# First batch turned on TensorE head by head, weight loads spread over it, last pair of each batch in halves

## The chip, the cores and the metric

The kernel runs on one core of a Trainium2 chip. The metric is the device time of one execution in microseconds; the median of three runs is compared. The core's engines work side by side, each through its own queue in order: PE (TensorE), DVE (VectorE), ACT (ScalarE), POOL (GpSimd) and SP (SyncE, which here only issues DMAs).

## The reference

Clustered attention, and behind it a gated feed-forward layer (FFN) on the attention's output:

```python
# q, k, v: (4 batches, 8 heads, 768, 64); centroids: (8, 16, 64)
q_assign = argmax(normalised q . normalised centroids)      # 16 clusters per head
k_assign = argmax(normalised k . normalised centroids)
mask   = q_assign[:, :, :, None] == k_assign[:, :, None, :]
scores = where(mask, q @ k.T / 8, -1e9)
attn   = softmax(scores) @ v
x      = attn, heads side by side                           # (3072 tokens, 512)
out    = (sigmoid(x @ w_gate) * (x @ w_val)) @ w_out         # d_ff = 1536
```

## The kernel before

**Operands.** For each head the kernel wants a tile `T` that holds k and q turned, features down the partitions and tokens along the row: six chunks of 128 keys and six of 128 queries. Each value is split in a high fp16 part and a low one (tile `hl`: DVE casts, then DVE or POOL subtracts), and both parts are turned together. From `T` PE computes the tokens' products with the centroids (`logits`, `logits2`); DVE picks the largest of the 16 and writes a one-hot row (`pick`, tile `oh`); the one-hots are turned too and placed in rows 64 to 79 of `T`, over the low part, with -1920 at the clusters a query is not in. A score matmul of 80 rows then contains the mask.

**Steps.** A step is one block of 128 keys against 384 queries of a head: `do_scores` (line 419: one matmul; line 424: the exponential on ACT), and two steps later (`LA = 2`) `do_av`, three matmuls of 65 columns (line 436). There are 96 steps in a batch, 384 in all. After a head's last step `normalise` divides (DVE, then POOL), and after a pair of heads the result `x` is turned by a DMA into `xT`, the input of the FFN.

**What runs between steps.** `at(i, f)` books preparation at step i, and it is issued in program order behind that step. Batches 1 to 3 are prepared by `pair_prep`, with DMA transposes of `hl` and of the one-hots and DMA copies (`hop`) that place them.

**The first batch before the change.** It is done in two passes of 48 steps: "A" takes all keys and the first 384 queries of every head, "B" the other 384 queries. So the first half of the batch's tokens is ready for the FFN after 48 steps (it starts 12 steps later). `a_split`, `a_turn` (DMA transpose, line 222), `a_logits`, `a_pick` and `a_place` prepare A, `b_split` to `b_place` prepare B. Before the first step 26 dummy matmuls (line 489) run on PE.

**The FFN** is a queue of atoms: 12 pairs of gate and value (lines 301 and 316, four matmuls of 384 columns each, booked at 643 ns apiece) and 9 output atoms (line 333, four matmuls of 512 columns, 864 ns) for each half batch of 384 tokens, which comes to 24 x 643 + 9 x 864 = 23,208 ns. `ffn_run(ns)` issues atoms until its credit is used. Before, the credit per step is the backlog, less a reserve of 7,000 ns, over the steps that are left in the batch:

```python
ffn_run(max(0.0, backlog() - reserve) / (total - done))
```

FFN weights come as float32 and are cast by POOL's DMAs: eight of gate and value, two of output. They are issued at steps 14, 26, 30, 34 (two each), 40 and 46.

**PSUM** has a ring of four banks (scores, logits, gates, values), two for `av`, two for the FFN's output.

Of the kernel before, what the change touches and what calls it, by code (L numbers as in the profile page):

```python
# [16 lines left out]
def kernel(  # L17
# [55 lines left out]


    ident = const.tile([128, 128], FP, name="ident")
    make_identity(nc, ident)
    identh = const.tile([128, 128], HP, name="identh")
    warm = const.tile([128, 512], HP, name="warm")
    POOL.memset(warm, 0.0)
    ones = const.tile([128, 128], HP, name="ones")  # L80
    POOL.memset(ones, 1.0)
# [9 lines left out]
    RAW = {}  # L91
# [6 lines left out]
    load(SP, "k", 0, 0)  # L98
    load(ACT, "q", 0, 0)
    SP.dma_start(out=cen, in_=centroids.rearrange("h c d -> (h c) d"))  # L100
    load(SP, "k", 0, 1)
    load(ACT, "q", 0, 1)
# [9 lines left out]
    def load_w(i):  # L112
        for t, src in ((wg[i], moe_w_gate), (wv[i], moe_w_val)):
            POOL.dma_start(
                out=t.rearrange("p dc fc f -> p dc (fc f)"),
                in_=src.rearrange("(dc p) (g f) -> p dc g f", p=128, f=WQ * 128)[:, :, i, :],
            )
# [15 lines left out]
    def centroid_a():  # L133
        DVE.tensor_tensor(sq, cen, cen, ALU.mult)
        DVE.tensor_reduce(ss, sq, AX.X, ALU.add)
        ACT.activation(r0, ss, AF.Sqrt)
        ACT.activation(r1, warm[:, 0:1], AF.Exp)

    def centroid_b():
        DVE.tensor_scalar(r0, r0, 1e-6, None, ALU.add)  # L140
        DVE.reciprocal(r0, r0)
        for i in range(2):
            DVE.tensor_scalar(c2[:, i, :], cen, r0, None, ALU.mult)
        ct_ps = bank(128, name="ct_ps")
        PE.transpose(ct_ps, c2.rearrange("p a d -> p (a d)"), ident)
        cv = ct_ps.rearrange("p (h c) -> p h c", c=NCL)
        ACT.copy(cm[:, :, 0, :], cv)
        DVE.tensor_tensor(cm[:, :, 1, :], cv, cm[:, :, 0, :], ALU.subtract)
# [4 lines left out]
    def v_cast(b, p):  # L153
        va = vap.tile([128, 2, NCH, 65], HP, name="va")
        VA[b, p] = va
        POOL.memset(va[:, :, :, 64:65], 1.0)
        POOL.tensor_copy(va[:, :, :, 0:64], RAW["v", b, p])
# [110 lines left out]
    ohs = [const.tile([128, NCH, 128], HP, name=f"oh{i}") for i in range(3)]  # L268
# [23 lines left out]
    def ffn_atoms(xT, t0, n, b, ch):  # L292
# [34 lines left out]
        def outp(t, part, st):  # L327
            def f():
                if part == 0:
                    st.append(op.tile([128, DM], FP, name="o"))  # L330
# [65 lines left out]
    def head_steps(b, p, e, kind):  # L396
        h = 2 * p + e
        if kind == "all":
            t, halves = T[b, h], [(T[b, h], 6), (T[b, h], 9)]
        elif kind == "A":  # L400
            t, halves = T["A", h], [(T["A", h], 6)]
        else:
            t, halves = T["A", h], [(T["B", p], 3 * e)]
        steps = []
        for j in range(NCH):
            for i, (tq, qo) in enumerate(halves):
                steps.append(dict(
                    b=b, p=p, e=e, nq=3 * len(halves), k=t[0:80, j, :],
                    q=tq[0:80, qo : qo + 3, :], j=j, c0=3 * i,
# [17 lines left out]
    def do_av(s, xT):  # L427
# [13 lines left out]
        if last:  # L441
            normalise(av, nq, b, p, e, x[:, :, bass.ts(e, 64)])
            if e == 1:
                SP.dma_start_transpose(
                    out=xT[:, p, :].rearrange("p (c t) -> p c t", t=128),
                    in_=x.rearrange("p c t -> p (c t)"),
                )
# [13 lines left out]
    def run_steps(heads, xT, reserve, xt_ready, lag=8):  # L461

        pend = []
        total = sum(n for n, _ in heads)
        done = 0
        for n, th in heads:
            for s in th():
                do_scores(s)
                pend.append(s)
                if xt_ready and done == lag:  # L470
                    xt_ready()
                if xt_ready and done < lag:
                    ffn_run(backlog() / (lag - done + 1))
                else:
                    ffn_run(max(0.0, backlog() - reserve) / (total - done))
                if len(pend) > LA:
                    do_av(pend.pop(0), xT)
# [3 lines left out]
        while pend:  # L481
            ffn_run(150)
            do_av(pend.pop(0), xT)


# [5 lines left out]
    ahl = {}  # L491

    def a_split(h, eng):
        k_, q_ = RAW["k", 0, h // 2], RAW["q", 0, h // 2]
        ahl[h] = split(9, [(0, k_[:, h % 2]), (6, q_[:, h % 2, 0:3])], eng)

    def a_turn(h):
        turn(("A", h), ahl[h], tp)

    def a_groups(h, side):  # L500
        return [(T["A", h], c, h) for c in (range(6) if side == 0 else range(6, 9))]

    st0 = {}

    def first_logits(e, oh):
        lg = logits2(a_groups(e, 0) + a_groups(e, 1))
        pick(lg, [(0, 6, 1, True, oh_view(oh, 2 * e, 1, 1, 6)),
                  (6, 9, 1, False, oh_view(oh, 2 * e + 1, 1, 1, 3))])

    def first_place(e, oh):  # L510
        ps = bank(NCH * 128, HP, name="oh_ps")
        for c in range(NCH):
            PE.transpose(ps[64 * e : 64 * e + 64, bass.ts(c, 128)], oh[:, c, 64 * e : 64 * e + 64], identh)
        t = T["A", e]
        pv = ps.rearrange("p (c t) -> p c t", t=128)
        DVE.tensor_copy(t[64:80, 0:6, :], pv[64 * e : 64 * e + 16, :, :])
        ACT.copy(t[64:80, 6:9, :], pv[64 * e + 32 : 64 * e + 48, 0:3, :])

    def a_logits(p):
        st0["lg", p] = logits2(sum((a_groups(2 * p + e, s) for s in range(2) for e in range(2)), []))  # L520

    def a_pick(p):
        oh = st0["oh", p] = new_oh()
        pick(st0["lg", p], [(0, 12, 2, True, oh_view(oh, 0, 2, 2, 6)),
                            (12, 18, 2, False, oh_view(oh, 1, 2, 2, 3))])

    def a_place(p):
        ps = oh_turn_pe(st0["oh", p], NCH)
        ot = ohp.tile([128, NCH, 128], HP, tag="ohT", name="ohT")
        DVE.tensor_copy(ot.rearrange("p c t -> p (c t)"), ps)  # L530
        for e in range(2):
            hop(ot, 2 * e, T["A", 2 * p + e], 0, 6)
            hop(ot, 2 * e + 1, T["A", 2 * p + e], 6, 3)

    def b_split(p):
        q_ = RAW["q", 0, p]
        st0["bhl", p] = split(6, [(0, q_[:, 0, 3:6]), (3, q_[:, 1, 3:6])], POOL)

    def b_turn(p):
        turn(("B", p), st0["bhl", p], tbp)  # L540

    def b_logits(p):
        st0["blg", p] = logits2([(T["B", p], c, 2 * p + c // 3) for c in range(6)])

    def b_pick(p):
        oh = st0["boh", p] = new_oh()
        pick(st0["blg", p], [(0, 6, 2, False, oh_view(oh, 0, 2, 1, 3))])

    def b_place(p):
        ps = oh_turn_pe(st0["boh", p], 3)  # L550
        ot = ohp.tile([128, 3, 128], HP, tag="ohT", name="ohT")
        DVE.tensor_copy(ot.rearrange("p c t -> p (c t)"), ps[:, 0:384])
        for e in range(2):
            hop(ot, e, T["B", p], 3 * e, 3)

    dummies(8)
    centroid_a()
    a_split(0, DVE)
    a_turn(0)
    a_split(1, POOL)  # L560
    a_turn(1)
    DVE.tensor_copy(identh, ident)
    centroid_b()
    for i in range(3):
        POOL.memset(ohs[i], 0.0)
    load(POOL, "v", 0, 0)
    load(SP, "k", 0, 2)
    load(SP, "q", 0, 2)
    a_split(2, POOL)
    load(POOL, "v", 0, 1)  # L570
    a_split(3, POOL)
    a_turn(2)
    a_turn(3)
    load(SP, "k", 0, 3)
    load(SP, "q", 0, 3)
    dummies(14)
    oh0 = new_oh()
    first_logits(0, oh0)
    dummies(2)
    first_logits(1, oh0)  # L580
    dummies(2)
    first_place(0, oh0)
    v_cast(0, 0)
    first_place(1, oh0)
    a_split(4, POOL)
    a_split(5, POOL)
    load(POOL, "v", 0, 2)
    load(POOL, "v", 0, 3)
    v_sum_pe(0, 0)

    at(0, lambda: a_logits(1))
    at(1, lambda: a_pick(1))
    at(3, lambda: a_place(1))
    at(4, lambda: (a_turn(4), a_turn(5)))
    at(5, lambda: v_cast(0, 1))
    at(6, lambda: v_sum_pe(0, 1))
    at(7, lambda: a_split(6, POOL))
    at(8, lambda: a_split(7, POOL))
    at(9, lambda: (a_turn(6), a_turn(7)))
    at(12, lambda: a_logits(2))  # L600
    at(13, lambda: a_pick(2))
    at(14, lambda: load_w(0))
    at(15, lambda: a_place(2))
    at(16, lambda: v_cast(0, 2))
    at(17, lambda: v_sum_pe(0, 2))
    at(22, lambda: a_logits(3))
    at(23, lambda: a_pick(3))
    at(25, lambda: a_place(3))
    at(24, lambda: v_cast(0, 3))
    at(26, lambda: v_sum_pe(0, 3))  # L610
    at(26, lambda: load_w(1))
    for p in range(NP):
        s = 20 + 7 * p
        at(s, lambda p=p: b_split(p))
        at(s + 3, lambda p=p: b_turn(p))
        at(s + 14, lambda p=p: b_logits(p))
# [102 lines left out]
```

## Time and profile before

| | |
|---|---|
| median of 3 runs | 379.2 us (379.12 to 381.24) |
| span of the profiled execution | 378.3 us |
| PE busy | 337.0 us, 89% |
| ACT, DVE, POOL busy | 230.4, 176.7, 113.6 us |
| mean granted TensorE clock | 0.932 |
| first score matmul | at 21.1 us |
| first score matmul of batches 1, 2, 3 | at 111.6, 170.9, 247.7 us |
| last score matmul | at 319.4 us |

The profiled execution has no time of its own beside its span; the span lies 0.9 us under the median, so 0.9 us is taken for what lies around it. Busy time of PE is time in which a matmul was under way, not time at PE's full rate: at a granted clock of 0.50 the same matmul takes about twice as long, so a busy stretch at that clock does half the work.

### The profile page before, as it was taken

How to read it: one execution, taken by the hardware profiler on the slowest of the kernel's cores; microseconds unless marked ns; L12 is line 12 of the kernel's file. 1: busy time of each engine (PE TensorE's matmuls, PEld its weight loads, DVE VectorE, ACT ScalarE, POOL GpSimd, SP SyncE). 2: the span in 40 equal slices, each digit the busy share in tenths (PEclk: the TensorE clock that was granted, in tenths of full speed). 3: DMA queues.
4: the chain of work that ended last, by engine and by line, in shares of the span. 5: the costliest groups of instructions: out<-in, count | busy, mean ns of one | idle time of the engine just before them, and what ended most of it. 6: DMA issues, size and time to landing. Idle time of an engine off the chain costs nothing.

```text
span 378.3 us, 8520 instructions
## 1 busy us (share of the span) xinstructions
PE 337.0 (89%) x3177; PEld 205.5 (54%) x3177; DVE 176.7 (47%) x455; ACT 230.4 (61%) x527; POOL 113.6 (30%) x179
## 2 busy tenths in 40 slices
PE   3786955669999989889999999999999999999995
PEld 1354633436655556554666566656665566565552
DVE  3463532225563675662656365635563333242230
ACT  3044744437867878875787778758777787232231
POOL 3756566103342634523242423232401000000000
PEclk9975875559999999999999999999999999999999
DMA  5967999974766976966566539653523120300102
GB/s 186 253 187 150 226 179 197 239 137 144 110 175 143 215 187 126 224 165 174 146 148 177 114 88 231 178 139 81 87 52 73 51 36 2 105 1 30 55 2 83
DMA packets 96858, 50.07 MB, mean 132 GB/s; under 512 B 75376, under 2 KB 93424, under 8 KB 96816
## 3 DMA queue, kind: packets, MB, share of 16 engines
q1 hardware_dynamic: 90032, 42.44, 48.0%
q0 software_dynamic: 6240, 6.29, 9.6%
q10 hardware_dynamic: 544, 0.79, 0.6%
q8 instruction: 25, 0.41, 0.4%
q14 instruction: 17, 0.14, 0.1%
HBM read 28.34 MB, written 6.29 MB: 92 GB/s over the span
## 4 chain that ended last, share of the span: by engine, by line
PE 68%; DMA 14%; DVE 7%; issue 4%; POOL 3%; ACT 1%; SPq 1%; POOLq 0%; DVEq 0%
PE o L333 16%; PE v L316 15%; PE g L301 15%; DMA T<-hl 12%; PE sc L419 11%; PE av L436 6%; PE lg L238 2%; DMA T<-ohT 2%; PE wm L489 2%; DMA cen<-in_centroids_dram 1%; DVE hT L321 1%; POOL hl L215 1%; DVE vs L163 1%; DVE hl L212 1%; DVE t L197 1%
## 5 line engine op out<-in xcount | busy, mean ns | idle before, releaser
L424 ACT ACTIVATE es<-sc 128x384 f16<-128x384 f32 x384 | 174.2, 492 | 67.6 <-PE sc L419 54.5
L419 PE MATMUL sc<-T 80*128 80x384 f16 x384 | 124.3, 348 | 5.8 <-DMA T<-ohT 4.5
L436 PEld LDWEIGHTS <-es 128*128 128x128 f16 x1152 | 84.6, 102 | 51.0 <-ACT es L424 6.1
L436 PE MATMUL av<-va,es 128*128 128x65 f16 x1152 | 102.3, 200 | 1.4 <-ACT es L424 0.7
L321 DVE SCALAR_TENSOR_TENSOR hT<-th,v 128x384 f16<-128x384 f32 x96 | 53.0, 552 | 94.8 <-PE av L436 56.1
L202 POOL TENSOR_TENSOR xp<-t,rec 128x384 f16<-128x384 f32 (+1 forms) x40 | 28.3, 707 | 146.2 <-DVE rec L199 119.2
L333 PE MATMUL o<-wo,hT 128*128 128x512 f16 x288 | 70.3, 378 | 0.0
L307 ACT ACTIVATE th<-g 128x384 f32<-128x384 f32 x96 | 47.2, 492 | 28.5 <-DVE hT L321 16.2
L301 PE MATMUL g<-xTb,wg 128*128 128x384 f16 x288 | 58.6, 325 | 0.5 <-DVE hT L321 0.2
L316 PE MATMUL v<-xTb,wv 128*128 128x384 f16 x288 | 58.6, 325 | 0.3 <-DVE hT L321 0.3
L301 PEld LDWEIGHTS <-wg 128*128 128x128 f16 x384 | 37.7, 98 | 24.0 <-issue 3.8
L316 PEld LDWEIGHTS <-wv 128*128 128x128 f16 x384 | 37.5, 98 | 22.7 <-issue 2.5
L333 PEld LDWEIGHTS <-hT 128*128 128x128 f16 x288 | 27.8, 97 | 26.1
L419 PEld LDWEIGHTS <-T 80*128 80x128 f16 x384 | 38.3, 100 | 5.4 <-DMA T<-ohT 4.2
L632 POOL TENSOR_TENSOR hl<-kraw,hl 128x384 f16<-128x384 f32 x24 | 22.0, 917 | 31.4 <-issue 24.8
L197 DVE TENSOR_TENSOR t<-av,sv 128x390 f32<-128x390 f32 (+1 forms) x40 | 19.2, 479 | 22.9 <-PE av L436 22.9
L632 POOL TENSOR_TENSOR hl<-qraw,hl 128x384 f16<-128x384 f32 x24 | 21.9, 913 | 20.7 <-DVE hl L631 20.5
L342 ACT ACTIVATE ob<-o 128x512 f32<-128x512 f32 x16 | 9.6, 597 | 22.6 <-PE o L333 22.4
L163 DVE TENSOR_REDUCE vs<-vraw 128x128 f16<-128x768 f32 x12 | 17.6, 1466 | 0.0
L340 DVE TENSOR_SCALAR ob<-o 128x512 f32<-128x512 f32 x8 | 5.5, 692 | 25.6 <-PE o L333 25.6
L252 DVE TENSOR_TENSOR lgs<-lg,lglo 128x192 f32<-128x192 f32 x24 | 8.5, 355 | 17.8 <-ACT lglo L244 17.3
L229 PE MATMUL lg<-cm,T 128*128 128x16 f16 x192 | 6.5, 172 | 10.9 <-DMA T<-hl 10.9
(68 smaller groups left out, 241.8 us busy)
## 6 DMA issues: line engine op xcount, KB each, us to landing
kraw<-in_k_dram SPq DMA_DIRECT2D x16, 384.0 KB, 3.9
out_dram<-ob SPq DMA_DIRECT2D x24, 256.0 KB, 2.1
qraw<-in_q_dram SPq DMA_DIRECT2D x14, 384.0 KB, 4.1
vraw<-in_v_dram SPq DMA_DIRECT2D x12, 384.0 KB, 5.4
vraw<-in_v_dram POOLq DMA_DIRECT2D x4, 384.0 KB, 4.4
wg<-in_moe_w_gate_dram POOLq DMA_DIRECT2D x4, 384.0 KB, 8.2
wv<-in_moe_w_val_dram POOLq DMA_DIRECT2D x4, 384.0 KB, 9.6
wo<-in_moe_w_out_dram POOLq DMA_DIRECT2D x2, 768.0 KB, 13.6
```

The lines of the kernel that those rows point to most:

```text
L163: DVE.tensor_reduce(s[:, :, 0:64], RAW["v", b, p].rearrange("p h c d -> p h d c"), AX.X, ALU.add)
L197: DVE.tensor_tensor(t[:, 0:nq, :], av, sv, ALU.add)
L202: (eng or POOL).tensor_tensor(x, t[:, 0:nq, 0:64], bcast(rec[:, 0:nq], 64), ALU.mult)
L301: PE.matmul(out=g[:, 0:n], lhsT=wg[fc // WQ][:, dc, fc % WQ, :], rhs=xT[:, dc, t0 : t0 + n], start=(dc == 0), stop=(dc == NDC - 1),)
L307: ACT.activation(th[:, 0:n], g[:, 0:n], AF.Tanh, scale=0.5)
L316: PE.matmul(out=w[:, 0:n], lhsT=wv[fc // WQ][:, dc, fc % WQ, :], rhs=xT[:, dc, t0 : t0 + n], start=(dc == 0), stop=(dc == NDC - 1),)
L321: DVE.scalar_tensor_tensor(hT[:, fc, 0:n], st[0][:, 0:n], 1.0, w[:, 0:n], ALU.add, ALU.mult)
L333: PE.matmul(out=o, lhsT=hT[:, fc, bass.ts(t, 128)], rhs=wo[fc // 6][:, fc % 6, :], start=(fc == 0), stop=(fc == NFC - 1),)
L419: PE.matmul(out=sc.rearrange("p (c t) -> p c t", t=128), lhsT=s["k"], rhs=s["q"], start=True, stop=True,)
L424: ACT.activation(es, sc, AF.Exp, scale=SCALE)
L436: PE.matmul(out=av[:, s["c0"] + i, :], lhsT=s["es"][:, bass.ts(i, 128)], rhs=VA[b, p][:, e, s["j"], :], start=(first and i == 0), stop=(la ...
L632: POOL.tensor_tensor(hl[:, :, 64:128], r, hl[:, :, 0:64], ALU.subtract)
```

## The change

- **First batch.** No A and B passes. Every head of batch 0 gets its 12 steps with all 768 queries, as in the other batches. `pieces(p, e)` prepares a head: casts on DVE, the low part on POOL (`hi`, `lo`), 12 PE transposes in two PSUM tiles (`tu`), DVE copies to `T` (`ev`), 24 logit matmuls (`lg`), the pick (`pk`), six PE transposes of the one-hots (`ot`), and two DVE writes straight into rows 64 to 79 (`pl`). The table `OFF` says how many steps ahead of the head each is issued. The PSUM tiles come from the two banks of the FFN's output, which is idle until late in this batch.
- **Start.** Pair 0 is loaded by heads, and head 0 is prepared in two parts of three chunks; its steps are ordered so that the first three need only the first part. Centroids are loaded first, on ACT's queue; all other loads of the batch go to SP's. 7 dummy matmuls instead of 26.
- **Weights** are issued one DMA at a time, every 10 steps from step 8 on, the output weights at 88 and 98.
- **Last pair of each batch** is done in halves (queries 0 to 383 of both heads, then the rest, 6 steps each), so that the first half of the tokens is complete at step 84 and its FFN is queued at step 92; the second half's FFN is queued at step 8 of the next batch.
- **Pacing.** Each step gives the FFN 500 ns of credit; there is no reserve, and the FFN halves are queued one behind the other (`ffn_block`), not interleaved (`ffn_two`). The last two steps' `av` of a batch now follow the first scores of the next.

```diff
+    def pieces(p, e, parts=1):
...
+        def tu(s, part=0):
+            a, z = rng(s, part)
+            ps = st["ps", s, part] = (
+                turns(name="t_ps") if parts == 1 else bank(128 * (z - a), HP, name="t_ps")
+            )
+            for c in range(a, z):
+                PE.transpose(ps[:, bass.ts(c - a, 128)], st["hl"][:, c, :], identh)
...
+        def pl(s, eng=None, part=0):
+            a, z = rng(s, part)
+            src = st["oh", part][-s][64 * e + 32 * s : 64 * e + 32 * s + 16, 0 : 128 * (z - a)]
+            dst = T[0, h][64:80, a:z, :].rearrange("p c t -> p (c t)")
+            if s == 0:
+                DVE.tensor_copy(dst, src)
+            elif eng is ACT:
+                ACT.activation(dst, src, AF.Copy, scale=MASK)
+            else:
+                DVE.tensor_scalar(dst, src, MASK, None, ALU.mult)
...
+    OFF = dict(hi0=-30, lo0=-30, hi1=-28, lo1=-28, tu0=-21, ev0=-20, tu1=-19, ev1=-18,
+               lg=-15, pk=-14, ot=-10, pl0=-9, pl1=-7)
+    W0, WS = 8, 10
...
+    for i in range(4):
+        for j in range(2):
+            at(W0 + WS * (2 * i + j), lambda i=i, j=j: load_w(i, j))
+    at(W0 + WS * 8, lambda: load_wo(0))
+    at(W0 + WS * 8 + 10, lambda: load_wo(1))
...
-    run_steps(heads(0, "A", 6), xA, 0, None)
-    run_steps(heads(0, "B", 6), xB, 6000, lambda: ffn_block(xA, 0, 384, 0, [0, 1, 2]), lag=12)
...
+                if second and done == LAG:
+                    second()
+                if done == 84 + LAG:
+                    first()
+                ffn_run(FFN_NS)
...
+    LAG = 8
+    FFN_NS = 500.0
...
+    def heads(b):
+        out = [(12, lambda p=p, e=e: head_steps(b, p, e, [0, 1])) for p in range(NP - 1) for e in range(2)]
+        return out + [
+            (6, lambda e=e, c=c: head_steps(b, NP - 1, e, [c])) for c in range(2) for e in range(2)
+        ]
...
+    CH = [[0, 1, 2], [3, 4, 5]]
+    prev = None
+    for b in range(B):
+        xT = xtp.tile([128, NDC, S], HP, tag="xTb", name="xTb")
+        half = lambda i, xT=xT, b=b: ffn_block(xT, 384 * i, 384, b, CH[i])
+        run_steps(heads(b), xT, prev, lambda: half(0))
+        prev = lambda half=half: half(1)
```

In batch 0 the last pair's `x` is turned by PE as well (`turn_x`), five steps after its `av`; elsewhere by DMA as before.

## The prediction

> **What bounds the kernel now.** I read the slices of the page first, then the six stages, then the chain, then PE's rows in the first batch. Slices (9.46 us each):
>
> ```profile
> PE   3786955669999989889999999999999999999995
> ACT  3044744437867878875787778758777787232231
> PEclk9975875559999999999999999999999999999999
> DMA  5967999974766976966566539653523120300102
> ```
>
> PE is full from slice 9 to the end at a granted clock of 9 and more. Before that it is half idle, and half of that time at half clock, while the DMA row is full in slices 4 to 7. So there are two kernels: a PE-bound one from about 85 us on, and a first batch bound by something else. The stages (start, batch 0 in its two passes, batches 1, 2, 3, tail); after the colon-pair come its length, then busy us of PE, PEld, DVE, ACT, POOL, the granted clock, DMA share and GB/s:
>
> ```profile
> 21.10:68.70 47.60, 30.57 (x379) 21.72 (x379) 19.02 (x62) 23.44 (x50) 28.30 (x45) 0.64 1.04 186
> 68.70:111.60 42.90, 38.06 (x372) 24.01 (x370) 21.13 (x63) 27.58 (x64) 10.71 (x17) 0.80 0.72 160
> 111.60:170.90 59.30, 53.00 (x613) 33.44 (x610) 35.51 (x93) 48.21 (x118) 24.45 (x36) 1.00 0.77 178
> 170.90:247.70 76.80, 75.90 (x756) 47.03 (x757) 42.68 (x106) 56.73 (x132) 24.68 (x36) 1.00 0.62 151
> 247.70:319.70 72.00, 71.64 (x688) 44.18 (x685) 31.82 (x74) 54.75 (x127) 14.64 (x23) 1.00 0.33 68
> 319.70:378.30 58.60, 54.78 (x309) 29.39 (x307) 16.28 (x30) 16.01 (x32) 0.83 (x1) 1.00 0.13 45
> ```
>
> Batches 2 and 3 and the tail are PE-bound (75.90 of 76.80, 71.64 of 72.00). Batch 0 takes 90.5 us, more than batch 2, though batch 2 carries 46.4 us of FFN and batch 0 only 17.2 (23.2 less the 6.0 it leaves). The chain names what stands there:
>
> ```profile
> 39.10 4.37 DMA T<-ohT
> ...
> 58.23 21.27 DMA T<-hl x2
> ```
>
> PE waits for DMA-turned operands, in the stretch in which the weights are issued. Last, what the half clock costs and what ends it:
>
> ```profile
> 37.70:41.10 3.40, 3.40 (x30) 2.48 (x29) 1.29 (x4) 2.17 (x5) 0.66 (x1) 0.50 1.26 168
> 41.20:44.60 3.40, 2.64 (x63) 2.12 (x62) 1.88 (x7) 2.10 (x6) 2.33 (x5) 1.00 1.02 228
> 68.40:71.80 3.40, 3.40 (x37) 2.34 (x37) 1.33 (x5) 2.18 (x5) 0.56 (x1) 0.50 1.21 196
> 71.90:75.30 3.40, 2.07 (x26) 1.41 (x25) 1.24 (x5) 1.57 (x4) 0.76 (x2) 0.50 1.14 294
> ```
> ```profile
> 39.78 0.51 PE L419 MATMUL sc<-T 80*128 80x384 f16 x1
> 40.27 0.51 PE L419 MATMUL sc<-T 80*128 80x384 f16 x1
> ...
> 68.36 0.49 PE L229 MATMUL lg<-cm,T 128*128 128x16 f16 x12 [4.64 <-DMA T<-hl]
> 68.71 0.80 PE L419 MATMUL sc<-T 80*128 80x384 f16 x2
> ...
> 69.99 0.51 PE L283 MATMUL oh_ps<-identh,oh 128*128 128x128 f16 x3
> 70.29 0.53 PE L419 MATMUL sc<-T 80*128 80x384 f16 x1
> ```
>
> At half clock a step of one score and three `av` matmuls costs PE 0.49 us (39.78 to 40.27), 12 logit matmuls 0.35 (68.36 to 68.71), three transposes 0.30 to 0.32 (69.99 to 70.29, a score behind them), so 0.105 each. At full clock the same steps follow each other every 0.385 us (scores at 46.67, 47.05, 47.44, 47.82 in the timeline), which is ACT's pace: seven exponentials in 2.89 us.
>
> **The change part by part.**
>
> *Batches 1 to 3 and the tail.* FFN per batch becomes 2.0 us (four steps of 500 ns from step 92) carried back, and 44.4 of the two halves in the batch: 46.4 in each of batches 1, 2 and 3. That is what batch 2 carries now (7.0 taken over, 46.4 queued, 7.0 left), so batches 1 and 2 get its row, 76.8 each, and batch 3 its own, 72.0 (no later batch to prepare). Batch 1 thus grows by 17.5. At the end 21.2 + 23.2 = 44.4 are left instead of 53.4: the tail is 58.6 - 9.0 = 49.6. The x of the last pair's first half must land between its `av` (issued at step 85) and the gate at step 92. The way is 0.36 + 0.18 + 0.52 (rows L197, L199, L202 for 3 chunks) and 3.1 for the DMA, 4.2 us, against four steps of 0.75 and three of 0.39, 4.2 us: I take nothing, and 1 us in each of three batches as the worse end.
>
> *The start (21.1 now).* The 5.75 us of dummies in the chain and the DMA turns go. New chain: centroids land at 5.65 now as the third DMA of SP, and come first on another queue: 5.1. Squares and sum 0.45, cast 0.35 (5.9); reciprocal 0.30, low part in two halves 0.35 each (6.9; POOL's two at 0.57 lie beside it); turn and evacuate two tiles of three, 0.5 + 0.36 x 2 (8.0); centroid tiles 0.29 x 2 (8.6); 12 logits 0.35 (8.9); pick 0.26 + 0.20 x 2 (9.6); six transposes 0.63 and their drain 0.2 (10.4); place 0.36 (10.8). Ten hand-overs at 0.07 make 11.5. ACT's own list (table load 1.28, two copies 0.47, v's cast, bounded by POOL's 0.84) ends at about 9.9, below it. Bounds: 10.5 and 14 (loads of pair 0 not before today's 6.0, and none of the hand-overs hidden). SP now issues 14 loads in a row at about 0.5 each, 7 us, ahead of its first transpose, which is not due before step 25: free.
>
> *Batch 0 on PE, at half clock.* 96 steps x 0.49 = 47.0. Turns of seven heads, 84 x 0.105 = 8.8; one-hots, 48 x 0.105 = 5.0; logits, 7 x 0.70 = 4.9; v's sums, 4 x 0.63 = 2.5 (38.65 to 39.28 in the timeline); batch 1's logits, 4 x 0.46 = 1.8 (288 in 11.0 us); x, three transposes 0.3. Sum 70.3. ACT needs 96 x 0.41 = 39 and lies beside it. DVE: six heads of casts 0.9, evacuations 1.12, pick 0.86, place 0.55 + 0.69, normalise 0.75 and half of sv 0.15, 5.0 each, 30; rests of heads 0 and 1, 7; batch 1's casts, picks and first v sum, 10 x 0.45 + 4 x 1.42 + 1.76 = 12: 49 of 70. POOL: 12 + 10 subtractions at 0.91, x 6.6, v 4, weights and zeros 9: 40. Both have room; at PE's full clock DVE would be the tightest. What DMA loses (12 turns of `hl`, 20 small copies) is gone from PE's waits, not moved: 15.4 us of waits of PE for batch 0's own turns (10.9 on `T<-hl`, 4.5 on `T<-ohT`). The weights, issued every 10 steps, land 8.2 to 9.6 us later (page, DMA issues); the last gate and value at step 78 is due about step 120, the output weights of steps 88 and 98 about step 123. If that cover were gone, PE would wait up to 13.6 us for `wo`. The last pair's x is turned at five steps behind its `av`, 3.6 us, for 1.1 us of DVE and POOL; only scores stand behind it.
>
> *Does PE stay at half clock?* It is at half clock at step 0: 7 dummies are 3.0 us (8 took 3.59), and the start then has gaps. Both windows of 3.40 us above are full of PE. Behind the one, which holds scores, `av` and a v sum, the clock is 1.00; behind the other, which also holds 12 logits and three transposes, it is 0.50. Of a head's 8.8 us at half clock 2.6 are logits and transposes, more than in the second window (0.65 of 3.40, 19%, against 30%), so by that row a full PE doesn't open the gate while heads are being prepared. Preparation ends at step 77; seven steps without any follow, 3.4 us, and the clock should open at about step 82. That takes 0.1 off 12 steps, 1.2, and gives the four FFN atoms their full-clock price, 16 x 0.163 = 2.6. So batch 0 is 70.3 - 1.2 + 2.6 = 71.7. The other end: if transposes count, PE fills a window early, the clock opens, and the batch runs at DVE's and ACT's pace: 12 us for the first 12 steps, in which DVE has 8.8 us of work and PE is still slow, then 84 x 0.53 = 45: 57.
>
> The Trainium skill, "TensorE: Matmul & The Clock Gate", section "Part 4: PE-mode transpose", speaks against this change: in transpose mode PE does not count as busy in the same way, and the full clock does not engage. By that rule batch 0 stays in the slow case; by a gate that counted transposes as any matmul it would be the 57. The row of 68.40 agrees with the rule, but logits stand in it as well, so the trace does not separate the two.
>
> **Sum.** 11.5 + 71.7 + 76.8 + 76.8 + 72.0 + 49.6 = 358.4; with 0.9 outside the span 359.3, say 359, against 379.2: 5% faster. Against now: start -9.6, batch 0 -18.8, batch 1 +17.5, tail -9.0.
>
> **The rivals.**
> 1. *The clock opens early in batch 0* (57 instead of 71.7): 345. For it: PE is nearly full there once prepared operands no longer come by DMA, and 41.20 shows the clock held at 2.64 of 3.40. Against it: 68.40.
> 2. *DMA still late.* Batch 1's turns of `hl` are issued at steps 47 to 95 among weights, loads and x, and the 21.27 us of the chain come back in part: half is 370, all of it 380. For it: 4.7 MB of loads, 3.2 of weights and 2.9 of turns in some 60 us are 180 GB/s, near the 186 of the stretch now. Against it: weights at half of today's density.
> 3. *Slower: DVE's queue is taken in order, and so is PE's.* Each head needs PE, DVE, PE, DVE, PE, DVE: turn 0.63, evacuate 0.56, logits 0.70, pick 0.86, turn 0.63, place 1.24. If this chain is not hidden behind steps but exposed, it is 4.6 us for each of seven heads, 32 us: 391. The point from which it decides is 2.9 us a head (20 us in seven). For it: DVE has 49 us of work in this batch and must not be late once; a logit bank in the ring of four holds up scores until DVE has read it. Against it: `OFF` puts 9 steps (4 to 6 us) between subtraction and turn and 2 to 4 between the links.
> 4. *The change doesn't do what it says*: the halves of the last pair let only 2.0 us of FFN into their own batch. That is in the sum already, and a first batch without FFN is paid for in batch 1.
>
> **How the numbers follow.** Forecast 0.54, rival 1 0.27, rival 2 0.11, rival 3 0.08. The likeliest time is 359, its own range 352 to 367 (start 10.5 to 14, 3 us of x, some exposure of heads). The range for 8 in 10 reaches down over rival 1 (345 less 3) and up over half of rival 2: 342 to 373. A measurement of this kernel tells about 1%, 3.8 us, from no change. Faster by more: the first two cases and half of rival 2, 0.87; same, rival 2 in full and a part of rival 3, 0.06; slower 0.07.
>
> **What would show it.** First score at 11 to 13 us; batch 0 some 72 us long with a granted clock of 0.50 to about step 80 and PE nearly full; no DMA into `T` before batch 1; batches 1 and 2 at 76 to 78 us each with PE full; last score 49 to 50 us before the end. Wrong would be a batch 0 over 91 us (the forecast's break-even), a clock that falls in batch 1, or PE waiting for `xTb` at step 92 by more than 1 us.

## The result, and the profile after

The changed kernel takes 352.25 us (median of four runs, 351.25 to 353.12) against 379.16 for the kernel before: a ratio of 0.928, 95% interval 0.9245 to 0.9315. The forecast was 359.0 with a range of 342 to 373. The profiled execution took 351.25 us, its span is 349.5. Medians are of all runs of a kernel; ratios, here and below, are to the kernel before as it was measured beside that run, and leave out the few executions that were over 1.5% slower than the fastest of the same kernel.

The slices of the page, 8.74 us each:

```profile
PE   7899987898999999999999999999999999999995
ACT  6478766776768876787768866787768766531330
PEclk9699989899999999999999999999999999999999
DMA  7968999999357735767468536951542002101002
```

PE is now nearly full from the first slice on. The clock row (granted TensorE clock, in tenths of full speed) has a 6 in the second slice and an 8 in the sixth and eighth; the fives that the first batch had are gone. The stages (start, batch 0, batches 1, 2, 3, tail; behind each stretch its length, busy us of PE, PEld (TensorE's weight loads), DVE, ACT and POOL with their instructions in brackets, the granted clock, the DMA share and GB/s):

```profile
0.00:9.60 9.60, 6.22 (x51) 3.43 (x51) 4.99 (x20) 6.04 (x11) 4.65 (x16) 1.00 0.76 243
9.60:71.40 61.80, 55.52 (x771) 38.81 (x771) 43.95 (x119) 43.12 (x102) 38.23 (x51) 0.89 0.99 210
71.40:149.00 77.60, 75.61 (x756) 46.53 (x754) 42.68 (x112) 56.79 (x133) 26.05 (x39) 1.00 0.72 162
149.00:226.00 77.00, 75.43 (x752) 46.33 (x749) 42.00 (x111) 56.72 (x133) 25.02 (x38) 1.00 0.65 151
226.00:300.30 74.30, 73.41 (x697) 44.74 (x696) 33.09 (x81) 54.98 (x128) 14.97 (x25) 1.00 0.30 69
300.30:349.50 49.20, 45.14 (x262) 24.76 (x260) 14.66 (x27) 13.93 (x28) 0.51 (x1) 0.98 0.10 35
```

Batch 0 went from 90.5 to 61.8 us, the start from 21.1 to 9.6, the tail from 58.6 to 49.2; batch 1 took over FFN work and grew from 59.3 to 77.6. The clock of batch 0 is 0.89; the forecast had 0.50 to about step 80. The trace has it at full from 6.54 to 9.96, so at step 0 (9.56) too, at half from 9.96 to 16.78, and at full again from there (the clock "opens" when it goes from half to full). Three windows around that opening:

```profile
9.90:13.40 3.50, 3.44 (x43) 2.55 (x42) 2.44 (x6) 1.87 (x4) 3.02 (x4) 0.51 1.06 384
13.40:16.80 3.40, 3.40 (x41) 2.91 (x39) 1.60 (x6) 1.07 (x3) 0.00 (x0) 0.50 1.08 374
16.80:20.20 3.40, 3.14 (x59) 2.22 (x57) 3.02 (x8) 2.40 (x6) 1.90 (x3) 1.00 0.74 260
```

The window from 13.4 is full of PE, with 12 transposes and ten logit matmuls among its 41 instructions, and the clock behind it is 1.00. Steps 0 to 11 take 10.1 us, the next 36 steps 19.4 (6.6, 6.1, 6.7), the last 48 steps 32.3. In these the clock falls twice for 3.4 us, at 47.5 and 61.2, each time after a window in which PE had been short of work (busy for 76% and 58% of it). The chain (the work that ended last, each piece with its start and length) has two landings of batch 1's operands there, at 45.80 and 68.28, and PE's waits in batch 0 (in all, times, longest) have two lines above 1 us that bear on it:

```profile
39.35 6.45 DMA T<-hl
...
62.74 5.54 DMA T<-hl
```
```profile
PE lg L257 <- DMA T<-hl: 1.5, 2, 0.8
PE sc L434 <- DVE T L596: 1.3, 1, 1.3
```

The first landing lies in the window ahead of the first fall. The second comes behind the second fall; ahead of that one stands the 1.3 us wait, at 59.3, for the write of a one-hot by DVE (line 596).

### The profile page after: what moved, and what is told of

The parts are those of the page before. It is cut to its first block, busy times and chain, and to the rows that moved or that the text cites. A ratio compares the mean times of both kernels' runs of the same rounds, so it can differ in the third digit from the quotient of the medians.

```text
span 349.5 us, 8661 instructions
## 1 busy us (share of the span) xinstructions
PE 331.3 (95%) x3272; PEld 204.6 (59%) x3272; DVE 181.4 (52%) x465; ACT 231.6 (66%) x531; POOL 109.4 (31%) x170
## 4 chain that ended last, share of the span: by engine, by line
PE 76%; DVE 9%; DMA 7%; issue 3%; ACT 2%; POOL 1%; POOLq 0%; ACTq 0%; DVEq 0%
PE o L351 17%; PE v L334 17%; PE g L319 15%; PE sc L434 13%; PE av L451 9%; DMA T<-hl 6%; PE lg L257 2%; DVE hT L339 2%; DVE vs L182 2%; ACT es L439 2%; PE t_ps L545 1%; DVE t L216 1%; DVE hl L679 1%; POOL hl L534 1%; PE lg L248 1%
## 5 line engine op out<-in xcount | busy, mean ns | idle before, releaser
L434 PE MATMUL sc<-T 80*128 80x384 f16 x384 | 120.7, 334 | 2.5 <-DVE T L596 1.3
L451 PEld LDWEIGHTS <-es 128*128 128x128 f16 x1152 | 81.5, 99 | 57.1 <-ACT es L439 13.6
L451 PE MATMUL av<-va,es 128*128 128x65 f16 x1152 | 99.7, 196 | 2.5 <-DVE hl L679 0.6
L319 PE MATMUL g<-xTb,wg 128*128 128x384 f16 x384 | 78.6, 325 | 1.6 <-DVE xTb L471 0.4
L334 PE MATMUL v<-xTb,wv 128*128 128x384 f16 x384 | 78.1, 325 | 1.4 <-DVE hT L339 1.4
L351 PE MATMUL o<-wo,hT 128*128 128x512 f16 x288 | 71.3, 378 | 0.0
L434 PEld LDWEIGHTS <-T 80*128 80x128 f16 x384 | 37.6, 98 | 1.4 <-DVE T L592 0.5
L680 POOL TENSOR_TENSOR hl<-qraw,hl 128x384 f16<-128x384 f32 x24 | 21.9, 912 | 11.0 <-DVE hl L679 10.9
L257 PE MATMUL lg<-cm,T 128*128 128x32 f16 x288 | 11.0, 177 | 2.3 <-DMA T<-hl 2.3
L176 POOL CAST va<-vraw 128x768 f16<-128x768 f32 x15 | 13.1, 872 | 0.0
```

What stands on the lines that cost most here:

```text
L319: PE.matmul(out=g[:, 0:n], lhsT=wg[fc // WQ][:, dc, fc % WQ, :], rhs=xT[:, dc, t0 : t0 + n], start=(dc == 0), stop=(dc == NDC - 1),)
L334: PE.matmul(out=w[:, 0:n], lhsT=wv[fc // WQ][:, dc, fc % WQ, :], rhs=xT[:, dc, t0 : t0 + n], start=(dc == 0), stop=(dc == NDC - 1),)
L351: PE.matmul(out=o, lhsT=hT[:, fc, bass.ts(t, 128)], rhs=wo[fc // 6][:, fc % 6, :], start=(fc == 0), stop=(fc == NFC - 1),)
L434: PE.matmul(out=sc.rearrange("p (c t) -> p c t", t=128), lhsT=s["k"], rhs=s["q"], start=True, stop=True,)
L451: PE.matmul(out=av[:, s["c0"] + i, :], lhsT=s["es"][:, bass.ts(i, 128)], rhs=VA[b, p][:, e, s["j"], :], start=(first and i == 0), stop=(la ...
L680: POOL.tensor_tensor(hl[:, :, 64:128], r, hl[:, :, 0:64], ALU.subtract)
```

## The experiments

Three questions: does a PE that transposes open its clock (the step on which forecast and result differ); which parts of the change carry the 27 us; and what still holds batch 0 up. The parts undone one by one are the even issue of the weights, the turns on PE and the halves. The single pass, the new start and the pacing without a reserve were not, so what each of them is worth stays open; and since the parts lean on each other, the losses below don't add up to 27.

### A full PE of three kinds, ahead of the first batch

The 7 dummy matmuls give way to a stream of about 10 us at half clock: 96 transposes, 24 matmuls of 512 columns, or 352 matmuls of 16 columns. Each was run once, and only the clock is read from it.

```diff
-    dummies(7)
+    wt = bank(128, HP, name="wt")
+    for i in range(96):
+        PE.transpose(wt, warm[:, 0:128], identh)
```

Transposes:

> The 7 dummy matmuls ahead of the first batch give way to 96 PE transposes of 128x128 in a row, about 96 x 0.107 = 10.3 us at half clock; everything else stays. Theory A (a PE that is full opens the clock, whatever fills it, as the changed kernel's stretch 13.40:16.80 suggests, full with 12 transposes, logits and scores and followed by clock 1.00): the granted clock goes to 1.00 within 3.4 to 6.9 us of the first transpose, from when on transposes follow each other at about half their distance, and the stream ends near 8 us. Theory B (the forecast's: transposes do not count): the clock stays at 0.50 to the end of the stream, at about 12 us, and opens only after it.

Wide matmuls:

> Control: 24 dummy matmuls of 512 columns in a row (24 x 0.427 = 10.2 us at half clock) in place of the 7. Both theories: the clock opens 3.4 to 6.9 us after the first one; the distance of two matmuls then falls from 0.427 to about 0.216, and the stream ends at 7 to 9 us.

Narrow matmuls:

> 352 matmuls of 16 columns in a row (the form of the logits, about 0.03 us apart: 10.2 us) in place of the 7 dummies. Theory A in its strong form (any instruction on PE counts): the clock opens 3.4 to 6.9 us after the first. Theory A in a weaker form (columns that stream count: 16 columns of 0.03 us are some 0.4 of PE's rate at half clock): it stays at 0.50 to the end. Theory B: it stays at 0.50.

The number of the stream's matmuls that are under way in a window of 1 us (in brackets), and their distance in time, measure the clock. Transposes:

```profile
4.00:5.00 1.00, 1.00 (x13) 1.00 0.80 244
5.00:6.00 1.00, 1.00 (x14) 1.00 1.00 336
6.00:7.00 1.00, 1.00 (x22) 1.00 0.96 346
```

Wide:

```profile
3.00:4.00 1.00, 1.00 (x4) 1.00 0.81 197
6.00:7.00 1.00, 1.00 (x7) 1.00 1.03 329
```

Narrow:

```profile
6.00:7.00 1.00, 1.00 (x44) 1.00 1.08 347
10.00:11.00 1.00, 1.00 (x44) 1.00 1.05 386
```

The number behind the brackets is the granted clock, and it reads 1.00 here from the start: ahead of the first change on record the profile shows full clock, whatever PE runs at, so the counts decide. Transposes started at 1.82 us at 0.107 us from each other and ran at 0.056 from 5.75 on, 3.9 us later, in a stream that held nothing else. Wide matmuls went from 0.427 to 0.216 at 4.5 us, 3.2 us after the first. Theory A holds for transposes, and theory B falls. The narrow stream is at 44 in every window, 0.027 us apart; that says little by itself, since logits of this width are 0.025 apart at full clock in the changed kernel. But the first clock change on record in that kernel is the opening at 27.67 us, head 0's transposes at 16.2 to 17.0 us are still 0.107 apart, and steps 0 to 11 took 10.5 us, so it had not opened before; PE was full of the narrow matmuls from 1.3 to about 7.2 us. So what narrow matmuls alone leave open is whether a longer stream without a break would do; a window full of them did not.

How far can one window be trusted? In all twelve traces the changes of the clock lie multiples of 3.41 us apart (47.50, 50.92, 61.16 and 64.57 in the changed kernel). Of the windows between these times in the first 110 us of each trace, 40 are at half clock with PE busy for at least 99.5%, not counting the one of narrow matmuls alone (ahead of a trace's first change, which is always to full, the clock counts as half). Behind 36 of them the clock was full, behind 4 it was not. The row of 68.40 in the kernel before, on which the forecast leaned, is one of the four; the others are one of the wide stream's kernel (55.7) and two of the kernel with DMA turns (54.8 and 58.2). What sets these four apart is open: windows with as many transposes and logits opened.

### The weights issued in bunches again

```diff
-    for i in range(4):
-        for j in range(2):
-            at(W0 + WS * (2 * i + j), lambda i=i, j=j: load_w(i, j))
-    at(W0 + WS * 8, lambda: load_wo(0))
-    at(W0 + WS * 8 + 10, lambda: load_wo(1))
+    for i, s in enumerate((14, 26, 30, 34)):
+        for j in range(2):
+            at(s, lambda i=i, j=j: load_w(i, j))
+    at(40, lambda: load_wo(0))
+    at(46, lambda: load_wo(1))
```

> The changed kernel with the weight loads back at the steps of the kernel before (14, 26, 30, 34 with two each, 40, 46). If the even issue carries part of the gain (theory: dense weights crowd out batch 1's operand turns, as in the chain of before with 21.27 us): batch 0 grows from 61.8 by 4 to 12 us, the clock falls once more, time 356 to 364. If it was only the first batch's own operands that waited for DMA: batch 0 within 1.5 us, time 351 to 354.

Measured 359.72 us, ratio to the kernel before 0.9482 (0.9435 to 0.953): 7.5 us of the gain are gone. The stage of batch 0, one line of PE's waits in it, and the step of its chain:

```profile
9.20:81.70 72.50, 58.95 (x769) 41.49 (x769) 46.87 (x121) 44.16 (x102) 38.74 (x52) 0.86 0.96 201
```
```profile
PE lg L257 <- DMA T<-hl: 6.9, 3, 6.5
```
```profile
48.05 15.05 DMA T<-hl
```

Batch 0 grew by 10.7 us (the profiled execution is the slowest of the four). The weights collide with batch 1's operands: a turn lands 15 us after its issue, PE waits 6.5 us at once for such a turn, and the clock is at half for 20.5 us in three stretches instead of 6.8 in two after the beginning. So the even issue carries some 7.5 of the 27 us.

### The operands of heads 2 to 7 turned by DMA again

```diff
-    OFF = dict(hi0=-30, lo0=-30, hi1=-28, lo1=-28, tu0=-21, ev0=-20, tu1=-19, ev1=-18,
+    OFF = dict(hi0=-30, lo0=-30, hi1=-28, lo1=-28, dm=-24,
```

Here `dm` is a DMA transpose of the head's `hl` into `T`; the one-hots are still turned on PE.

> The changed kernel with the operands of heads 2 to 7 of the first batch turned by DMA again (issued four steps after the second subtraction, nine steps before the logits); head 0, head 1, the one-hots and all else stay as changed. Removes 72 PE transposes (72 x 0.055 = 4.0 us at full clock) and 12 evacuations (6.7 us of DVE), adds six DMA turns. Theory 1 (PE's turns are what pays): PE waits for the six turns, 1 to 2.5 us each, the clock falls more often, batch 0 +6 to +15 us. Theory 2 (the start, the single pass and the pacing pay; who turns is of no matter): batch 0 within 2 us, or shorter by up to 4.

Measured 368.51 us, ratio 0.967 (0.961 to 0.973): some 15 us of the gain are gone, by the ratios. Batches 0 and 1, and PE's waits from 9 to 100 us:

```profile
9.20:79.10 69.90, 59.67 (x698) 41.56 (x698) 40.67 (x109) 45.46 (x102) 38.24 (x51) 0.73 1.10 219
79.10:167.60 88.50, 78.13 (x755) 47.55 (x754) 42.81 (x112) 56.95 (x133) 26.02 (x39) 0.94 0.78 143
```
```profile
PE lg L257 <- DMA T<-hl: 9.5, 1, 9.5
PE lg L248 <- DMA T<-hl: 8.2, 4, 5.5
```
```profile
80.81 16.12 DMA T<-hl
```

Batch 0 is 8.1 us longer, as theory 1 had it, with 73 fewer PE instructions and 3.3 us less DVE work: saved work that buys nothing, because the turns land late (PE waits 8.2 us for them, L248) and the clock is 0.73. The rest is in batch 1, 10.9 us longer, where PE waits 9.5 us at once for an operand of batch 1 (L257 is the logits of later batches). That one is not shown to come from the six turns: the last of them had landed by 59.3, and the late turn was issued at 80.81. What stands beside it are the loads of the output weights of steps 88 and 98, which landed at 86.5 and 99.5. The same turn (booked at step 95) in all runs, in us:

| run | output weights at steps | that turn, issue to landing | first 12 steps of batch 1 |
|---|---|---|---|
| changed kernel | 88, 98 | 7.6 | 10.4 |
| w1_fill | 88, 98 | 9.3 | 12.2 |
| c2_wide, u2_whole | 88, 98 | 9.6, 9.6 | 12.5, 13.6 |
| c1_turns, x1_act | 88, 98 | 10.5, 10.6 | 13.7, 13.9 |
| c3_narrow | 88, 98 | 12.7 | 16.5 |
| u3_dma | 88, 98 | 16.1 | 20.0 |
| u1_dense | 40, 46 | 5.5 | 9.4 |
| v1_gap, v2_late (below) | 98, 106 | 5.0, 4.4 | 9.4, 9.5 |

Every run with these weights at 88 and 98 loses time at that turn, and no other run of the table does. No run moves these two loads alone, so that they are the cause is argued from the table and not shown; why the turn takes 7.6 us in one and 16.1 in another is open too.

### The last pair of each batch whole

```diff
-    FFN_NS = 500.0
+    FFN_NS = 530.0
...
-        run_steps(heads(b), xT, prev, lambda: half(0))
-        prev = lambda half=half: half(1)
+        run_steps(heads(b), xT, prev, lambda: None)
+        prev = lambda half=half: (half(0), half(1))
```

`heads` gives the last pair two heads of 12 steps, as the other pairs.

> The changed kernel without halves: the last pair of each batch runs head by head with 12 steps, both FFN halves are queued at step 8 of the next batch, and the credit is 530 ns a step instead of 500, so that 88 steps still carry 46.4 us. By the forecast's sums the halves move 2.0 us of FFN from the tail into the first batch and nothing else: time +1 to +3 us, tail 51 instead of 49.2. Rival (the halves matter more, since the FFN's queue runs dry for the first eight steps of each batch and PE has only scores and av): +5 to +9 us.

Measured 373.48 us, ratio 0.9815 (0.9754 to 0.9876): 20 to 21 us of the gain are gone, far over both expectations. Batch 0 is 59.9 us, but batches 1 to 3 take 83.2, 81.1 and 80.3 (77.6, 77.0 and 74.3 with halves) and the tail 57.9 instead of 49.2. Three windows at the beginning of batch 2:

```profile
152.00:156.00 4.00, 3.68 (x36) 1.73 (x36) 1.34 (x5) 4.00 (x11) 2.91 (x5) 1.00 1.09 295
156.00:159.00 3.00, 0.35 (x5) 0.29 (x5) 0.00 (x0) 0.15 (x1) 0.52 (x1) 0.97 0.74 141
159.00:162.20 3.20, 3.20 (x16) 1.61 (x14) 0.55 (x1) 1.47 (x3) 0.00 (x0) 0.50 0.72 109
```

and PE's waits in the tail and, of another kind, in batch 1:

```profile
PE g L319 <- DMA xTb<-xp: 4.1, 1, 4.1
```
```profile
PE lg L257 <- DMA T<-hl: 3.9, 1, 3.9
```

The FFN's queue is dry for the first eight steps of a batch, which then pass at ACT's pace (152 to 156: ACT 4.00 of 4.00). They take some 3 us, too little for the last pair's division and turn: the FFN's first gate matmul stands at the head of PE's queue and waits (156 to 159: PE 0.35 of 3.00), scores and all else behind it. And the clock halves for the next 3.4 us. It waits 2.7 us so in batch 2, 3.4 in batch 3 and 4.1 in the tail, which lose 4.1, 6.0 and 8.7 us. Batch 1, whose `x` came by PE, has no such wait; of its 5.6 us the 3.9 are the late turn of the table above. With halves there is a half of FFN in hand while the other half's operand is turned. (The kernel before had a reserve of 7,000 ns for the same purpose; this experiment has neither, so it does not say what halves would be worth beside a reserve.)

### A fuller start, moved weights, later logits

```diff
-    dummies(7)
+    dummies(8)
...
     a["pk"](0)
+    fill(1)
     a["ot"](0)
+    fill(2)
```

> The changed kernel with four more dummy matmuls in gaps of PE before step 0 (one more at the start, one between the logits and the turn of head 0's one-hots, two behind that turn), so that PE is full from 1.3 to about 9.6 us. If a full PE opens the clock, it is at 1.00 by step 0 and the cold stretch 9.96 to 16.78 goes: steps 0 to 11 take 7.5 to 9 us instead of 10.1, time -1 to -2.5 us (349.8 to 351.3). If transposes do not count, it stays cold to 16 us and the time is the same or up to 0.9 us longer, by what the dummies delay.

Measured 351.73 us, ratio 0.9269 (0.923 to 0.9309), not told apart from the changed kernel; the gain of 1 to 2.5 us was expected and did not come. Yet the start did what it should. First the changed kernel, then this one, each with the first 12 steps and the first 12 steps of batch 1:

```profile
9.60:19.60 10.00, 9.82 (x131) 7.55 (x131) 6.72 (x18) 4.74 (x11) 4.40 (x6) 0.66 1.01 357
71.40:81.80 10.40, 9.55 (x103) 6.25 (x101) 5.40 (x13) 7.43 (x18) 4.18 (x6) 1.00 1.16 196
```
```profile
9.00:17.40 8.40, 7.54 (x133) 5.70 (x132) 7.36 (x20) 4.68 (x11) 4.33 (x6) 1.00 1.06 375
68.70:80.90 12.20, 9.59 (x104) 6.29 (x103) 5.43 (x13) 7.46 (x18) 4.18 (x6) 1.00 1.27 181
```

The clock is full from 6.7 to 44 us, the first 12 steps take 8.4 instead of 10.1 us (8.4 also in both kernels below, which have this start; with the changed kernel's start they took 8.8 to 10.5 in u1_dense, u2_whole and x1_act, so a part of the 1.7 us varies from run to run). Batch 1 begins 2.7 us earlier, and its first 12 steps give 1.8 of that back: an operand turn that PE waits 2.6 us for, the one of the table. It lands at 79.6 us, against 80.5 in the changed kernel, so a faster PE waits longer for nearly the same landing.

So, on top of this start, the weights were moved to where DMA had room (v1_gap, below); and then the logits, pick and one-hot turn of later batches were also put two steps later (v2_late), so that an operand's turn has two steps more:

```diff
-    for i in range(4):
-        for j in range(2):
-            at(W0 + WS * (2 * i + j), lambda i=i, j=j: load_w(i, j))
-    at(W0 + WS * 8, lambda: load_wo(0))
-    at(W0 + WS * 8 + 10, lambda: load_wo(1))
+    for n, s in enumerate((8, 14, 20, 26, 32, 38, 64, 82)):
+        at(s, lambda i=n // 2, j=n % 2: load_w(i, j))
+    at(98, lambda: load_wo(0))
+    at(106, lambda: load_wo(1))
```

> The fuller start (four more dummies) and the weights moved to where DMA has room: gate and value at steps 8, 14, 20, 26, 32, 38, 64 and 82, output weights at 98 and 106. In the changed kernel DMA moves 122 to 125 GB/s from 17 to 35 us and 201 to 255 from 44 to 87, where batch 1's operands are turned. If DMA's crowding between steps 47 and 110 is what gave the fuller start's gain back: PE's waits for turned operands of batch 1 fall below 1 us, the first 12 steps of batch 1 take 9.5 to 10 us instead of 12.2, time 346.5 to 349.5. If batch 0's end is bound by DVE and POOL: 350.5 to 352.

Measured 350.64 us, ratio 0.9254 (0.9223 to 0.9284): the lowest of all, not distinguishable from the changed kernel, and in the second theory's range (350.5 to 352). The first 12 steps of batch 1 take 9.4 us, where 9.5 to 10 was expected of the first theory, but steps 48 to 59 take 8.8 instead of 7.3, and PE's waits for batch 1's operands are not below 1 us; 2.9 of these 3.3 us now lie in batch 0:

```profile
PE lg L257 <- DMA T<-hl: 3.3, 3, 2.2
```

> As the one with the moved weights, and the logits, pick and one-hot turn of batches 1 to 3 come two steps later, so an operand turn has 13 steps instead of 11 before its logits. If turns still land late after the move of the weights: 1 to 2 us less than it, and no falls of the clock in batch 0. If they land in time by then: the same within 0.5 us.

Measured 355.01 us, ratio 0.9374 (0.9346 to 0.9401): worse, which neither theory had.

```profile
PE t_ps L550 <- DVE T L561: 2.5, 3, 1.9
```

The waits for DMA are gone from PE's list, and these 2.5 us of waits for DVE's evacuations have come in (0.6 before); the clock falls three times. Batch 0 took 62.1 us, 0.5 more than with the weights moved alone; batches 1, 2 and 3 took 0.7, 1.1 and 1.3 more, for which no cause was found. That the moved picks meet the first batch's heads in DVE's queue is a guess from the waits.

### The last one-hot write on ACT

```diff
-                f = d[k_[:2]]
+                f = d[k_[:2]] if k_ != "pl1" else (lambda s_, d=d: d["pl"](s_, ACT))
```

> The changed kernel with the last write of each head's one-hots (the queries', 16x768, 0.56 us on DVE) moved to ACT, for heads 2 to 7. If DVE's queue in order holds up batch 0 (third rival, in small: one wait of 1.31 us for this write at 59.30, followed by a fall of the clock): time -0.5 to -2 us. If ACT paces the steps: each costs ACT about 0.8 us in front of exponentials, batch 0 +2 to +4.5 us.

Measured 356.97 us, ratio 0.9375 (0.9323 to 0.9427), with times from 352.2 to 357.5.

```profile
PE lg L257 <- DMA T<-hl: 5.1, 3, 4.0
```

Seven such writes (one of them half as wide) took 0.755 us each on ACT in the mean, and batch 0 grew by 1.4 us to 63.2. The larger part of the loss is elsewhere: the first 24 steps of batch 1 took 25.0 us instead of 20.5, with a wait of 4.0 at once for the turn of the table, so it is not shown to come from this edit. What the run does show is that relieving DVE of these writes by ACT did not shorten batch 0.

## Why the prediction was right, and where it was wrong

The direction, the order of size and the range held: 359 forecast, 352.25 measured. But the reason behind the 359 did not hold: the clock opened early, which is rival 1, given 0.27 against 0.54 for the forecast's own case. That the total still lies only 7 us under the 359 is in part luck: batch 0 came 9.9 us under its term and the start 1.9, while batch 3 and the time outside the span came 3.2 over theirs, and rival 1 alone would have given 345. Term by term, in us (measured: the profiled execution, 351.25):

| | forecast | measured |
|---|---|---|
| start | 11.5 | 9.6 |
| batch 0 | 71.7 | 61.8 |
| batch 1 | 76.8 | 77.6 |
| batch 2 | 76.8 | 77.0 |
| batch 3 | 72.0 | 74.3 |
| tail | 49.6 | 49.2 |
| outside the span | 0.9 | 1.75 |

**Batches 1 and 2 and the tail** were read from rows of the kernel before with the FFN's account moved, and came within 1 us. Batch 3 took 2.3 more; its window holds nine matmuls more than the row it was read from, and PE is busy for 1.8 us more (73.41 against 71.64), which is most of it.

**The step that failed is "Does PE stay at half clock?"** It said that a PE full of transposes and logits would not open the clock before about step 82. It opened at 16.8 us, in step 6, behind a window full of just these. (It was not at half clock at step 0 either, as that step began; it fell 0.4 us later.) The reason I gave was one window of one trace, and the transpose stream shows it wrong: 96 transposes alone opened the clock 3.9 us after the first. The Trainium skill, "TensorE: Matmul & The Clock Gate", section "Part 4: PE-mode transpose", which says that full clock does not engage in transpose mode, is contradicted by that run; the measurement decides. The same page's section "Part 1: The HAM clock gate (the "warmup" mystery)", by which about 3.4 us of sustained activity release the clock, is near the 3.2 and 3.9 us of the two streams. With the clock open, the alternative end of that step, 57 us (rival 1, 345 in all), was the nearer one: batch 0 is 4.8 us over it.

**Those 4.8 us** lie in the second half of the batch. The first 12 steps took 10.1 us, where the 57 allowed 12; steps 12 to 47, all at full clock, took 0.54 each, which is the pace of 0.53; the last 48 took 32.3 us, where that pace gives 25.4. In these 6.9 us stand the four FFN atoms (2.6 by the forecast's own price), the two stretches of 3.4 us at half clock, and waits: for batch 1's turns, 1.5 us, and for one late DVE write, 1.3. That is rival 2 and rival 3 in small. How much each costs was not measured apart: emptying DMA's early stretch, moving DVE's writes, or waking PE earlier each left the time where it was or made it longer, with a wait in another place.

**The start** was 1.9 us shorter. The centroids, first in their queue, landed 2.92 us after their issue, at 3.65; the sum had them at 5.1, from the landing of a third DMA, which is 1.4 of it. (Its terms, added again, make 11.6, not 11.5.) And what ended last was not the sum's chain but ACT's list, which the forecast had below it: the first score waits for ACT's write of the one-hots, which stood behind the cast of v there.

```profile
9.56 0.32 PE L434 MATMUL sc<-T 80*128 80x384 f16 x1 [1.00 <-ACT T L594]
```

**Rival 4** spoke of the halves as 2.0 us moved. The sum was right, since it took batch 2's row, where a reserve kept the FFN's queue from running dry. The reason given for the halves was not: without them, and without a reserve, 20 to 21 us are lost, some 3 of these in a wait that is not theirs.

**What DMA lost** was called gone from PE's waits, and is: with heads 2 to 7 turned by DMA, PE waits 8.2 us for them in batch 0. What the forecast missed is the turn beside the output weights: it asked when these would be needed (about step 123), and not which turn would be under way beside their loads at steps 88 and 98. In the changed kernel the first 12 steps of batch 1 are 1 us longer than in the runs without these loads there, in other runs with the same load steps up to 10.5 (20.0 against 9.4).

## What to carry to other kernels

Count transposes as work when asking for PE's clock, and narrow matmuls alone not; then look for the gaps: a wait of 1.3 us was followed by 3.4 us at half clock here. A stage with a full engine needs its next operand finished well before the old work runs out, so hand work over in halves or keep a reserve. When a large load is moved to a place where its own consumer has time, ask what else is in flight there that PE waits for. Before building a forecast on one window, look for a second that says the same, and where two ends lie 15 us apart, say what single run would decide between them.

## What was not expected of the hardware

- A stream of nothing but 128x128 transposes took the clock from half to full (0.107 to 0.056 us each), 3.9 us after its start.
- A window of 3.41 us full of 16-column matmuls did not; they came every 0.027 us.
- Ahead of the first clock change on record the profile's granted clock reads 1.00 while wide matmuls run at 0.427 us each; the distance of the matmuls is the safer reading there.
- How busy a window must be for the clock to hold is not one number: with PE busy for 57% of it a window held in one trace (c2_wide, from 79.6 us), with 78% the clock fell in another (w1_fill, from 40.8 us).
